# Chunk 3's decays loaded ahead of four second-layer weights, and the stored decays clipped on VectorE

## The chip, the cores and the metric

The kernel runs on one core of a Trainium2 chip. The metric is the device time of one execution in microseconds (us): 614.49 as the median of three runs (613.55, 614.49, 615.33). All arithmetic is in fp32.

The engines are named as in the profile: PE is TensorE (PEld its weight loads), DVE is VectorE, ACT is ScalarE, POOL is GpSimd, SP issues most DMAs. L625 is line 625 of the kernel before.

## The reference

The kernel computes a state-space scan over four batches of 768 positions with eight heads, and feeds its result to a layer of four gated experts. Cut to what matters here:

```python
def _attn_ref(x, a, B, C):                 # x (4, 8, 768, 32), a (4, 8, 768), B and C (4, 8, 768, 16)
    log_a = np.log(np.clip(a, 1e-06, 1.0))
    for c in range(nc):                    # chunks of the sequence
        cum = np.cumsum(la, axis=-1)
        L = np.exp(cum[:, :, :, None] - cum[:, :, None, :]) * causal
        M = np.einsum('bhin,bhjn->bhij', Cc, Bc) * L
        y = einsum('bhij,bhjd->bhid', M, xc) + einsum('bhin,bhnd->bhid', Cc, state) * exp(cum)
        state = exp(sum(la)) * state + sum_j(B_j x_j * exp(cum[-1] - cum_j))

def _moe_ref(x, domain_probs, w1, w2):     # x (3072, 256), w1 (4, 256, 1024), w2 (4, 1024, 256)
    p = domain_probs / (domain_probs.sum(-1, keepdims=True) + 1e-09)
    for e in range(E):
        out += p[:, e:e + 1] * (np.maximum(x @ w1[e], 0.0) @ w2[e])
```

`a` holds the decays that the change is about.

## The kernel before

**Tiles and stages.** The kernel works in 24 chunks of 128 positions. For each chunk it needs the matrix of decays between all pairs of positions of a head. For the first chunks this comes from a running product ("scan", L519): VectorE multiplies along the positions by the decay and adds a row of the identity. Chunks 0 to 2 spread the decays over the partitions by small matmuls into PSUM (L660) and scan from there. Chunks 3 to 5 (`c < SCANNED`) read the clipped decays from DRAM, broadcast to all 128 partitions into a 512 KB tile `ab` (`load_decays`, L463). From chunk 6 on, exponentials of cumulative sums take their place (L526). The scores of two chunks (L502, eight matmuls into four banks of PSUM) are multiplied by the decay matrices on VectorE (L856, one 128x512 product for each bank), and the outputs (L546, and L879 for the state carried from an earlier chunk) are matmuls on these products `MT`.

The expert layer follows on transposed outputs. Its products (L933) are 128x256 matmuls. The first four blocks of F use the weights as they are: `plain_first` (L1235) multiplies the first-layer weights, L968 evicts a bank through ReLU and gate, and `own_` (L1390) multiplies the second-layer weights. All other products go by schemes with fewer multiplications, for which sums of weights (L1024) are formed on GpSimd and VectorE, and sums of tokens (L1043) on VectorE.

**The beginning is written out by hand** (L560 to L738). It clips the decays of chunks 0 to 2 on VectorE (`aq0`, `aq1`), and all decays (`a_sb`, 96x256) on GpSimd. GpSimd then copies the clipped ones to `a_cut` and zeroes the first position of each row, and SP stores `a_cut` to DRAM as `acut_d` (L633). `a_sb` itself is needed later for the logarithm (L708). SP issues its DMAs in the order of the program: tokens, two first-layer weights, chunk 2's tokens, the store, chunk 3's tokens, two more first-layer weights, four second-layer weights, chunk 3's decays. The load of the decays reads what the store wrote, and SP waits for the store's completion before it issues it. A DMA also waits, at SP, for the one that last used its completion counter, some eight DMAs earlier.

**The rest is planned.** Everything from L742 on is handed to `Plan`, which walks through the work with estimated durations and sets the order of instructions on each engine. Matmuls keep the order in which the lists are written. The other engines take what is ready first by the estimates. The plan starts at `now = 13.2` us, and what the part by hand has begun enters it as "taken" with the time from which it can be used: the decays of chunk 3 (`st[3]["ab"]`, L777) at `now + 2`, the second-layer weights (L1350) at `now + 4 + fb`. Buffers, too, are given out by the plan. An instruction of GpSimd that would share a port with VectorE waits for the last two-input VectorE instruction written before it (L1515).

**The stage around the change.** TensorE's order from 12.6 us on: chunk 2's decays are spread into four banks (L660); two plain products (L933 x16 in the profile, which counts each fp32 matmul as two); a transpose of the cumulative sums (L1360); the scores of chunks 2 and 3 (L502), of which three of the four banks are banks that chunk 2's scan reads; two more plain products and the first of the second layer (L933 x24); the outputs of chunks 2 and 3 (L546). VectorE's order: four scans of chunk 2 from PSUM, an eviction L968, the first half of chunk 3's scan from `ab`, an eviction, the second half, then the four products L856 among two evictions.

Of the kernel before, what the change touches and what calls it, by code (L numbers as in the profile page):

```python
# [10 lines left out]
ALU = mybir.AluOpType  # L11
# [348 lines left out]
def kernel(  # L360
# [10 lines left out]
    nc = tc.nc  # L371

    NCH, _, W = xbc.shape
# [19 lines left out]
    def real(c):  # L393
        return c % NSEQ * NC + c // NSEQ
# [26 lines left out]
    def some(n, shape, name, pool=const):  # L421
        return [pool.tile(shape, FP32, name=f"{name}{i}") for i in range(n)]

    homes = {
        "V": some(NV - 4, [P, 2, FB], "v"),
        "W": some(NW, [P, 2 * FB], "w"),
        "bank": some(8, [P, 512], "bank", psum),
        "xb": some(4, [P, W], "xb"),
        "ab": some(2, [P, NH * P], "ab"),
        "ah": some(3, [HN, P], "ah"),  # L430
        "MT": some(2, [P, 2, NH, P + N], "MT"),
        "ctm": some(4, [HN, NT, P], "ctm"),
# [14 lines left out]
    st = {c: {} for c in range(NCH)}  # L447
# [13 lines left out]
    def load_decays(c, ab):  # L461
        src = acut_d if c < SCANNED else cum_d
        nc.sync.dma_start(  # L463
            out=ab, in_=src[real(c)].rearrange("h s -> (h s)").partition_broadcast(P))
# [10 lines left out]
    def load_w1(fb, w):  # L475
        e, f = divmod(fb, EPB)
        nc.sync.dma_start(
            out=w.rearrange("p (a f) -> p a f", a=2),
            in_=w1[e].rearrange("(a p) f -> p a f", a=2)[:, :, f * FB:f * FB + FB])

    def load_w2(fb, w):
        e, f = divmod(fb, EPB)
        nc.sync.dma_start(
            out=w.rearrange("p (j m) -> p j m", j=JJ),
            in_=w2[e, f * FB:f * FB + FB].rearrange("(j p) m -> p j m", p=P))
# [65 lines left out]
    def keep_state(c, A, y):  # L551
# [14 lines left out]
    a_sb = homes["cum"][0]  # L566
    a_cut = homes["V"][-4][:NCH * NH // 2, 0].rearrange("p (r s) -> p r s", r=2)
# [5 lines left out]
        out=aq0.rearrange("(q r) t s -> q r (t s)", q=NQ)[:, 0], in_=a_rows[:, 0])  # L573
    nc.scalar.dma_start(
        out=aq1.rearrange("(q r) c t s -> q r c (t s)", q=NQ)[:, 0], in_=a_rows[:, 1:SPREAD])
# [5 lines left out]
        out=a_sb, in_=a.rearrange("c h s -> (c h) s").rearrange("(p r) s -> p r s", r=2))  # L581
# [14 lines left out]
    for q in range(NQ):  # L596
        nc.vector.memset(tmask[32 * q:32 * q + N, 0:1], 1.0)
    nc.vector.tensor_scalar(out=tmask[:, 1:2], in0=tmask[:, 0:1], scalar1=-1.0, scalar2=1.0,
                            op0=ALU.mult, op1=ALU.add)
# [7 lines left out]
    def clip(engine, v, top=1.0):  # L607
        engine.tensor_scalar(out=v, in0=v, scalar1=1e-6, scalar2=top, op0=ALU.max, op1=ALU.min)
# [13 lines left out]
    clip(nc.vector, aq1.rearrange("p c t s -> p (c t s)"), own)  # L622
    nc.vector.memset(aq1[:, :, :, 0:1], 0.0)

    clip(nc.gpsimd, a_sb)  # L625
    nc.gpsimd.tensor_copy(a_cut, a_sb)
    nc.gpsimd.memset(a_cut[:, :, 0:1], 0.0)

    def store_decays(engine, d, sb):
        engine.dma_start(  # L630
# [3 lines left out]
    load_tokens(3, xb[3])  # L634
    for fb in range(2, 4):
        load_w1(fb, homes["W"][fb])
    for fb in range(4):
        load_w2(fb, homes["W"][4 + fb])
    load_decays(3, homes["ab"][0])

    BANK = homes["bank"]
    rows = NCH * E
# [81 lines left out]
    for r in range(2):  # L724
        nc.vector.tensor_tensor_scan(
            out=sums[:, r], data0=a_sb[:, r], data1=zeros[:NCH * NH // 2], initial=0.0,
            op0=ALU.add, op1=ALU.add)
# [14 lines left out]
    plan = Plan(homes)  # L742
    line = []
    B512, B256 = {"DVE": D512, "POOL": 1.3}, {"DVE": D256, "POOL": .72}
    now = 13.2
# [28 lines left out]
    for c, i in ((2, 2), (3, 3)):  # L774
        st[c]["xb"] = plan.taken("xb", i, now)
    st[2]["ctm"] = plan.taken("ctm", 0, now)
    st[3]["ab"] = plan.taken("ab", 0, now + 2)  # L777
    for c in range(2):
        st[c]["A"] = plan.taken("A", c, now)
    g0 = gates[0, 0] = plan.taken("gate", 0, now)  # L780
# [566 lines left out]
    loaded = {}  # L1347
    for fb in range(4):
        loaded[fb, 1] = plan.taken("W", fb, now + (0.0 if fb < 2 else 3.0))
        loaded[fb, 2] = plan.taken("W", 4 + fb, now + 4.0 + fb)  # L1350
    for (fb, l), v in loaded.items():
        weights["S", fb, l] = v

# [31 lines left out]
    for seq, _ in plain[2:]:  # L1385
        line.extend(seq)
    dma(lambda _: nc.sync.dma_start(
        out=g0.t[:, 4:6], in_=p_d[0, 4:6].rearrange("c s -> (c s)").partition_broadcast(P).rearrange(
            "p (c s) -> p c s", s=P)), kb=128, part=[g0])
# [174 lines left out]
```

## Time and profile before

| | |
|---|---|
| median of three runs | 614.49 us |
| the profiled execution's span | 615.3 us |
| TensorE busy | 605.7 us (98%) |
| VectorE busy | 489.5 us (80%) |
| ScalarE busy | 292.5 us (48%) |
| GpSimd busy | 157.6 us (26%) |
| mean granted TensorE clock | 0.997 |
| TensorE busy from 13.2 to 27.0 us | 11.74 of 13.80 us |
| TensorE busy from 27.0 to 50.0 us | 23.00 of 23.00 us |
| TensorE busy from 50.0 to 90.0 us | 38.43 of 40.00 us |
| TensorE busy from 90.0 to 605.0 us | 514.73 of 515.00 us |

The profile shows one execution. A row of its timeline has the start, the duration, the engine, the line and operation, the tiles (output, then inputs), the number of merged instructions, and in brackets how long the engine had been idle before it and what ended the idle time. A row of waits has the waiting engine and line, what released it, the sum in us, how often, and the longest. A released wait that names an engine which had long been done was for something else, often a DMA. SPq rows are the issues of DMAs by SP; when a DMA's parts have landed is in the trace as counts of its semaphore, up to 16 for each DMA.

### The profile page before, as it was taken

To read this page: it belongs to the slowest core of one execution; us is meant where nothing else is said; L and a number is where in the kernel's file an instruction comes from. 1 tells how busy PE (TensorE), PEld (TensorE's weight loads), DVE (VectorE), ACT (ScalarE), POOL (GpSimd) and SP (SyncE) were. 2 spreads that over 40 slices of the span, in tenths; PEclk is the share of its full clock that TensorE was granted. 3 is DMA by queue.
4 is the path that set the end of the run, shared out by engine and by line. 5 is a ranking of instruction groups with operands and counts; after the bars stand their busy time and mean duration, and the time that the engine had idled before them with its cause. 6 is when DMAs were issued, how large, how long until landed. Compare 5 with 4: busy or idle time off the path is not lost.

```text
span 615.3 us, 10136 instructions
## 1 busy us (share of the span) xinstructions
PE 605.7 (98%) x3365; PEld 514.8 (84%) x3365; DVE 489.5 (80%) x854; ACT 292.5 (48%) x681; POOL 157.6 (26%) x238
## 2 busy tenths in 40 slices
PE   9899999999999999999999999999999999999997
PEld 5677878888888888888888888888888888888885
DVE  7879897998969895697978988386785979576775
ACT  4237646378651327877443333844444242434441
POOL 5536556636372000776500100210000000000000
PEclk9899999999999999999999999999999999999999
DMA  7737578676863429983442424964233232964001
GB/s 249 256 114 231 204 218 300 205 224 208 280 188 94 134 34 285 297 291 146 132 144 77 137 63 118 284 222 137 61 111 87 93 90 51 303 230 126 1 0 52
DMA packets 89060, 99.65 MB, mean 162 GB/s; under 512 B 27428, under 2 KB 58928, under 8 KB 89008
## 3 DMA queue, kind: packets, MB, share of 16 engines
q1 hardware_dynamic: 88852, 98.95, 51.4%
q8 instruction: 27, 0.44, 0.3%
q14 instruction: 25, 0.20, 0.1%
q10 hardware_dynamic: 156, 0.06, 0.0%
HBM read 78.80 MB, written 20.17 MB: 161 GB/s over the span
## 4 chain that ended last, share of the span: by engine, by line
PE 92%; DVE 2%; ACT 1%; issue 0%; DVEq 0%
PE bank L933 88%; PE bank L546 2%; PE bank L502 1%; PE bank L879 1%; DVE v L960 1%; DVE v L968 1%; ACT A L556 1%; DVE MT L856 0%; ACT v L894 0%; DVE bank L1071 0%; DVE v L1260 0%; PE bank L1325 0%; DVE v L1425 0%; ACT LT L894 0%; ACT v L1330 0%
## 5 line engine op out<-in xcount | busy, mean ns | idle before, releaser
L933 PE MATMUL bank<-v,w 128*128 128x256 f32 x1716 | 402.0, 381 | 1.1 <-DVE bank L1071 0.8
L933 PEld LDWEIGHTS bank<-v,w 128*128 128x128 f32 x1716 | 325.7, 191 | 50.0 <-issue 2.9
L933 PE MATMUL bank<-Y,w 128*128 128x256 f32 x692 | 177.3, 381 | 0.7 <-ACT LT L894 0.4
L933 PEld LDWEIGHTS bank<-Y,w 128*128 128x128 f32 x692 | 130.2, 190 | 21.9 <-issue 1.7
L1213 ACT COPY v<-bank 128x512 f32<-128x512 f32 x109 | 63.9, 586 | 177.5 <-PE bank L933 165.2
L968 DVE SCALAR_TENSOR_TENSOR v<-bank,gate 128x512 f32<-128x512 f32 x147 | 101.0, 688 | 39.6 <-PE bank L933 36.8
L960 DVE TENSOR_TENSOR v<-v,v 128x512 f32<-128x512 f32 x179 | 125.9, 720 | 2.1 <-ACT v L942 0.8
L1024 POOL TENSOR_TENSOR w<-w,w 128x256 f32<-128x256 f32 x94 | 72.1, 784 | 46.0 <-DVE v L960 13.8
L1071 DVE TENSOR_TENSOR bank<-bank,v 128x512 f32<-128x512 f32 x81 | 55.5, 696 | 35.2 <-PE bank L933 23.6
L942 ACT COPY v<-bank 128x512 f32<-128x512 f32 x97 | 56.7, 587 | 55.0 <-PE bank L933 46.7
L947 ACT COPY bank<-v 128x512 f32<-128x512 f32 x126 | 73.2, 594 | 10.8 <-DVE v L968 8.7
L526 ACT ACTIVATE MT<-ab,neg 128x128 f32<-128x128 f32 x144 | 46.9, 393 | 2.0 <-DMA ab<-cum_d 2.0
L933 PE MATMUL bank<-LT,w 128*128 128x256 f32 x168 | 42.6, 380 | 0.0
L531 POOL TENSOR_SCALAR_AFFINE_SELECT MT<-MT 128x512 f32<-128x512 f32 x36 | 23.0, 652 | 67.8 <-ACT MT L526 53.9
L933 PEld LDWEIGHTS bank<-LT,w 128*128 128x128 f32 x168 | 31.8, 190 | 4.6 <-DVE v L968 0.3
L1024 POOL TENSOR_TENSOR w<-w 128x256 f32<-128x256 f32 x32 | 24.2, 762 | 23.2 <-DVE Y L1043 9.0
L960 DVE TENSOR_TENSOR v<-bank,v 128x512 f32<-128x512 f32 x26 | 17.9, 689 | 11.7 <-PE bank L933 9.9
L1260 DVE TENSOR_TENSOR v<-v,v 128x256 f32<-128x256 f32 x58 | 22.9, 431 | 1.1 <-ACT v L1213 0.7
L856 DVE TENSOR_TENSOR MT<-bank,MT 128x512 f32<-128x512 f32 x36 | 22.7, 681 | 0.1
L968 DVE SCALAR_TENSOR_TENSOR v<-v,gate 128x512 f32<-128x512 f32 x26 | 19.7, 758 | 0.4
L1213 ACT COPY LT<-bank 128x512 f32<-128x512 f32 x12 | 7.0, 586 | 23.5 <-PE bank L933 23.5
L840 POOL TENSOR_TENSOR cts<-ctm,dec 128x256 f32<-128x256 f32 x20 | 14.5, 734 | 11.6 <-DVE v L960 5.1
(110 smaller groups left out, 322.1 us busy)
## 6 DMA issues: line engine op xcount, KB each, us to landing
w<-w_d SPq DMA_DIRECT2D x128, 256.0 KB
w_d<-w SPq DMA_DIRECT2D x64, 256.0 KB
w<-in_w_dram SPq DMA_DIRECT2D x40, 256.0 KB
ab<-cum_d SPq DMA_DIRECT2D x18, 512.0 KB
w<-in_w_dram SPq DMA_DIRECT2D x64, 128.0 KB
gate<-p_d SPq DMA_DIRECT2D x15, 384.0 KB
xb<-in_xbc_dram SPq DMA_DIRECT2D x17, 192.0 KB
out_dram<-v SPq DMA_DIRECT2D x144, 16.0 KB
```

The lines of the kernel that those rows point to most:

```text
L526: nc.scalar.activation(out=MT[:, place(c, h), 0:P], in_=ab[:, h * P:h * P + P], func=AF.Exp, bias=neg[:, h % NT, NQ * real(c) + h // NT:NQ ...
L531: nc.gpsimd.affine_select(out=MT[:, h:h + n, 0:P], in_=MT[:, h:h + n, 0:P], compare_op=ALU.is_ge, fill=0.0, base=0, pattern=[[0, n], [1, P ...
L856: nc.vector.tensor_mul(to, g, LT0[:, js, h] if cs[0] < SCANNED else to)
L933: nc.tensor.matmul(out=o, lhsT=w[:, j], rhs=x if half is None else x[:, j], start=(start and j == 0), stop=(j == 1), skip_group_check=True)
L942: act(.5, lambda e: nc.scalar.copy(out=flat(v), in_=bank.t), reads=[bank], writes=[v])
L947: act(.54 if to - lo > FB else .32, lambda e: nc.scalar.copy(out=bank.t[:, lo:to], in_=flat(v)[:, lo:to]), reads=[v], writes=[bank])
L960: plan.add(engines, lambda e: (on(e).tensor_add if sign > 0 else on(e).tensor_sub)(flat(v), whole(x), whole(y)), reads=[x, y], writes=[v], ...
L968: dve(D512, lambda e: nc.vector.scalar_tensor_tensor(out=h.t, in0=whole(x).rearrange("p (j m) -> p j m", j=JJ), scalar=0.0, in1=g.t[:, 2 * ...
L1024: plan.add(B256, lambda e, r=r, x=x, y=y, sign=sign: (on(e).tensor_add if sign > 0 else on(e).tensor_sub)(view(r), view(x), view(y)), two= ...
L1071: dve(D512, lambda e: (nc.vector.tensor_add if sign > 0 else nc.vector.tensor_sub)(to.t, bank.t, whole(x)), reads=[x, bank], writes=[to])
L1213: act(.5, lambda e: nc.scalar.copy(out=flat(v), in_=bank.t), reads=[bank], writes=[v], hold=HOLD)
L1260: plan.add(engines, lambda e: (on(e).tensor_add if sign > 0 else on(e).tensor_sub)(o[1](), x[1](), y[1]()), reads=[v for v in vs if v is n ...
```

## The change

Four edits. The clip that makes `a_cut` is done on VectorE, straight from the raw decays, with the memset behind it, and GpSimd's clip in place comes after it; the copy goes. The load of chunk 3's decays stands ahead of the four second-layer weights in SP's order. In the plan, these decays are taken as there at `now` (13.2) and no longer at `now + 2`, and the second-layer weights at `now + 5 + fb` and no longer at `now + 4 + fb`.

```diff
@@ -622,9 +622,9 @@
     clip(nc.vector, aq1.rearrange("p c t s -> p (c t s)"), own)
     nc.vector.memset(aq1[:, :, :, 0:1], 0.0)
 
+    nc.vector.tensor_scalar(out=a_cut, in0=a_sb, scalar1=1e-6, scalar2=1.0, op0=ALU.max, op1=ALU.min)
+    nc.vector.memset(a_cut[:, :, 0:1], 0.0)
     clip(nc.gpsimd, a_sb)
-    nc.gpsimd.tensor_copy(a_cut, a_sb)
-    nc.gpsimd.memset(a_cut[:, :, 0:1], 0.0)
 
@@ -634,9 +634,9 @@
     load_tokens(3, xb[3])
     for fb in range(2, 4):
         load_w1(fb, homes["W"][fb])
+    load_decays(3, homes["ab"][0])
     for fb in range(4):
         load_w2(fb, homes["W"][4 + fb])
-    load_decays(3, homes["ab"][0])
 
@@ -774,7 +774,7 @@
     st[2]["ctm"] = plan.taken("ctm", 0, now)
-    st[3]["ab"] = plan.taken("ab", 0, now + 2)
+    st[3]["ab"] = plan.taken("ab", 0, now)
     for c in range(2):
@@ -1347,7 +1347,7 @@
     for fb in range(4):
         loaded[fb, 1] = plan.taken("W", fb, now + (0.0 if fb < 2 else 3.0))
-        loaded[fb, 2] = plan.taken("W", 4 + fb, now + 4.0 + fb)
+        loaded[fb, 2] = plan.taken("W", 4 + fb, now + 5.0 + fb)
```

With these numbers the plan puts VectorE's work of this stage in another order: the first half of chunk 3's scan from `ab` stands first, then two of chunk 2's scans, an eviction, the other two, an eviction, the second half of chunk 3's scan, and the four L856 among two evictions. GpSimd's first sum of weights, which waited for a VectorE sum of tokens, waits for the first half of chunk 3's scan. Later in the program neighbouring instructions change places on VectorE, ScalarE, GpSimd and SP; TensorE's order is the same, with other buffers.

## The prediction

> **What bounds the kernel now.** I read the share of each engine first, then what TensorE waited for from 13 us to the end, then the rows around the largest wait in order of time, then the busy time by stretches. The two lines from the page:
>
> ```profile
> PE 605.7 (98%) x3365; PEld 514.8 (84%) x3365; DVE 489.5 (80%) x854; ACT 292.5 (48%) x681; POOL 157.6 (26%) x238
> PE 92%; DVE 2%; ACT 1%; issue 0%; DVEq 0%
> ```
>
> TensorE is busy for 98% of the span and holds 92% of the chain that ended last. Its instructions and their order are the same in both kernels (804 rows each, buffer numbers apart), so the change can only alter its pauses. These are few:
>
> ```profile
> PE bank L546 <- POOL w L1024: 1.4, 1, 1.4
> PE bank L933 <- DVE bank L1071: 0.8, 1, 0.8
> PE bank L1325 <- DVE v L1260: 0.7, 1, 0.7
> PE bank L546 <- DVE MT L856: 0.7, 1, 0.7
> PE bank L933 <- ACT LT L894: 0.4, 1, 0.4
> PE bank L933 <- DVE v L968: 0.3, 1, 0.3
> ```
>
> Together 4.3 us, of which two rows of L546 (the outputs of chunks 2 and 3) make 2.1 us. These are what the change aims at, so no more than about 2.4 us can come from that place. The rows that lead to it:
>
> ```profile
> 6.35 0.34 SPq L630 DMA_DIRECT2D acut_d<-v  x1
> ...
> 11.23 0.47 SPq L463 DMA_DIRECT2D ab<-acut_d  x1
> ...
> 14.22 2.43 DVE L519 TENSOR_TENSOR_SCAN LT<-bank,ident 128x256 f32<-128x256 f32 x4
> ...
> 17.09 1.15 PE L502 MATMUL bank<-ctm,xb 32*128 32x256 f32 x16
> ...
> 18.17 5.45 PE L933 MATMUL bank<-v,w 128*128 128x256 f32 x24
> 19.13 1.23 DVE L519 TENSOR_TENSOR_SCAN LT<-ab,ident 128x512 f32<-128x512 f32 x1 [1.90 <-DMA ab<-acut_d]
> ...
> 25.34 0.68 DVE L856 TENSOR_TENSOR MT<-bank,LT 128x512 f32<-128x512 f32 x1
> ...
> 26.08 1.18 PE L546 MATMUL bank<-MT,xb 128*32 128x144 f32 x30 [0.70 <-DVE MT L856]
> ```
>
> Chunk 3's decays are issued at 11.23; VectorE sits idle for 1.90 us until they are there and scans at 19.13. From there it works without a gap (scan, two evictions with the scan's second half between, then four products L856 among two evictions) up to 26.02, and TensorE, ready at 18.17 + 5.45 = 23.62, starts the outputs in earnest at 26.08.
>
> **The change part by part.** Four edits.
>
> *VectorE clips the stored decays.* It adds a clip of 96x256 and a memset. Nearest rows: the clip of 128x256 at 3.22 took 0.35, the memset at 3.64 0.06. VectorE ends its own memset at 4.48 and idles 0.87 us until the scan at 5.35; the decays are there by 4.56 (the trace's landing records: the semaphore counts of the DMA engines). 4.6 + 0.4 = 5.0: hidden by that idle time, cost 0; without the cover 0.4. GpSimd loses a copy (0.39) and a memset (0.10); its own clip (1.07) now waits for VectorE's read, so it ends near 6.0 in place of 5.72, and its first reader, the logarithm, is at 8.98: cost 0, covered by 3 us.
>
> *The store of the decays* could leave SP at 5.85, where the load before it has been issued, in place of 6.35. This buys nothing: by the landing records its 16 parts land from 9.03 to 11.11, each about 0.3 us behind the load ahead of it (8.76 to 10.81), so it stands in a backlog, not on its issue.
>
> *The load is moved past four weight loads on SP.* It reads what the store wrote, so it waits for the store's 11.11. Before, SP reached it at 11.2 anyway; hence it is issued at about 11.2 in both kernels. What changes is what is ahead of it in the DMA queue: before, the four weights (the last lands at 16.35) and then the decays at 19.01; now only the first-layer weights, whose last part lands at 13.40. The landing L of the decays from both sides: other 512 KB loads of this trace land 1.2 to 2.7 us behind the transfer ahead of them, so 14.6 to 16.1; and those that found the queue nearly empty landed 3.5 (issued 288.90) to 5.1 us (265.92) after their issue, so 14.7 to 16.3. The most alike, issued with a transfer ahead that ends 2.5 us later (144.27 and 170.80), took 4.3 and 4.2. I take L = 15.4 and keep 14.6 to 16.3.
>
> The Trainium skill (DMA: Bandwidth & Descriptors, Anatomy of one DMA, fitted there on GpSimd's path) puts a DMA at some 2.0 us plus its bytes over 436 GB/s. By that the store would be done near 8.1 and the load issued there; for this store, issued at 6.35, the trace has 11.11. Since the load would still stand behind the first-layer weights, L by the page would be about 15, an estimate, and the gain 1.5 us in place of the 1.1 below.
>
> *The order on VectorE.* The planner is now told that the decays are there at 13.2, and puts the scan of their first half first, ahead of chunk 2's four scans from PSUM. That is a new wait: behind it stand the chunk 2 scans, and behind these TensorE, since the scores (L502) overwrite the banks that they read. Steps from the starts of the rows of before: landing to scan 0.12; scan 1.14; PSUM scan 0.585; eviction 0.58; second scan 1.49; L856 0.6.
> - VectorE: L + 0.12 + 1.14 + 2 x 0.585 + 0.58 + 2 x 0.585 + 0.58 + 1.49 + 2 x 0.6 + 0.6 + 0.6 + 0.68 = L + 9.35.
> - TensorE: the third scanned bank is free at L + 0.12 + 1.14 + 1.17 + 0.58 + 0.6 = L + 3.6. Five of the eight scores are left, 5/8 of 1.08, then 24 matmuls at 0.217 (a long stretch of L933 has 185.83 us for 860) make 5.2: the outputs can start at L + 9.5.
>
> Both paths are about equal; with 0.1 for the hand-over the outputs start at max(23.6, L + 9.6), that is 25.0 for L = 15.4, in place of 26.08: **1.1 us sooner** (1.9 to 0.2 over the bounds of L). Even is at L = 16.5.
>
> What else moves. SP has issued the first-layer weights by about 7.7 and now stands at the load's wait until 11.2; behind it stand four weight loads, two stores and the next tokens. The second-layer weights are issued at 11.7 to 13.5 in place of 8.23 to 11.19 and land some 2.5 us later (about 16 to 19); their first reader is the last third of the 24 matmuls, near 23 now; covered by 4 us or more. The store of the sums (12.63), the gates' store and the tokens of chunks 4 and 5 leave SP 0.5 to 1.4 us later; their readers (ACT's masks at 20.19, scores at 31.7) have cover, about 10 us up to the scores. GpSimd's first weight sum waited for a VectorE sum at 13.92 and started at 14.38; it now waits for the scan, until 16.75. Behind it stand the two L540 that the outputs need: five sums of 0.71, L540, the sum that waits for the second scan (L + 6.3 = 21.7), L540: done at 22.8, before 25.0; cost 0, and 2.2 us of cover.
>
> After this stage the plan is recomputed. On GpSimd and SP the same work is in nearly the same order; on VectorE neighbours change places. The next pauses (0.3 at 50.75, 0.8 at 77.31, 0.4 at 86.81) can shrink to nothing or double: -1.5 to +1.5, and I take 0. In the stretch from 50 to 90 us VectorE is the fullest:
>
> ```profile
> 50.00:90.00 40.00, 38.43 (x237) 31.52 (x237) 37.83 (x63) 23.16 (x68) 22.62 (x36) 1.00 0.70 216
> ```
>
> (columns: PE, PEld, DVE, ACT, POOL.) But the chain enters VectorE there at 68.36, released by a matmul, so an earlier TensorE lets it begin earlier, and the gain passes through.
>
> **The sum.** The profiled execution spans 615.3 us, 0.8 over the median of 614.49 and inside the runs shown (613.55 to 615.33). 615.3 - 1.1 = 614.2; against the median, 614.49 - 1.1 = **613.4**. Rounds of this kernel differ by 0.3% (1.8 us); below that I call it the same.
>
> **Rivals.**
> - *Faster: the later pauses go too.* With L = 14.6 the outputs gain 1.9; or the pauses at 77 and 50 us vanish besides the 1.1 (0.8 + 0.3). 614.5 - 2.2 = 612.3. For it: VectorE's products of chunks 4 and 5 come earlier in the new order (all four L856 ahead of two evictions). Against: VectorE's total work is unchanged and full in that stretch.
> - *Slower: the scan in front blocks chunk 2.* From L = 16.5 on TensorE's scores wait longer than the outputs did. If the decays land no sooner than before (19.0), the outputs start at 28.6, 2.5 us later than 26.08: 617.0. For it: this load took 7.8 us from issue to landing before, one at 77.28, with the queue almost empty, 6.65 (L = 17.9, +1.4), and the new order leaves nothing else for VectorE to do meanwhile. Against: 1 MB less is queued ahead.
> - *Given back.* VectorE is at 37.83 of 40 us from 50 to 90; if the new order makes it the bound there from 50 on, the 1.1 us are waited for again: 614.5. Against it: the release at 68.36 by TensorE.
> - *The load is not earlier at all* in its issue: that is my own forecast, and it is no rival for the time, since the queue ahead is what shrinks.
>
> **How the numbers follow.** Forecast as worked out (613.4; own range 612.6 to 614.3 by the bounds of L, up to 615.8 if later pauses grow by 1.5): 0.44. Given back (614.5): 0.08. Faster (612.3 and below): 0.30. Slower (617.0, from 616.3 on): 0.18. Same is the first two, 0.52. The range leaves out the far ends of the faster and the slower case, one in ten each: 611.7 to 616.6.
>
> **What would show it.** In the new trace: the L463 of chunk 3 issued near 11.2, not near 7.8 (else the store landed early); the first scan of `ab` on VectorE near 15.5; a new pause of TensorE at L502 of about 2 us, near 17 to 19, in place of those at L546; the outputs L546 starting at 25.0. It is wrong if the scan starts at 14 or before (then 2.4 us), if it starts after 16.5 (then slower), or if the pauses at 50 to 87 us change by more than 1 us in sum.

## The result, and the profile after

The changed kernel takes 617.46 us (median of 8 executions, 616.55 to 619.50) against 615.22 for the kernel before beside it (8 executions, 613.55 to 617.28): a ratio of 1.0038, interval 1.0021 to 1.0055. It is slower by 2.2 us, where 1.1 us less was forecast. A second comparison gave 617.32 against 614.89, ratio 1.0034 (1.0018 to 1.0050).

The profiled execution of the changed kernel spans 615.4 us, almost the 615.3 of before. From the waits of TensorE after the change (waiting engine and line, what released it, the sum in us, how often, the longest) the two rows of L546 are gone, and one of L502 has come:

```profile
PE bank L502 <- DVE LT L519: 1.0, 2, 0.6
PE bank L1325 <- DVE v L1260: 0.7, 1, 0.7
PE bank L933 <- ACT LT L894: 0.4, 1, 0.4
PE bank L933 <- DVE bank L1071: 0.3, 1, 0.3
```

TensorE pauses 1.9 us less than before, 2.4 in place of 4.3 by the rows shown, and yet nothing is won. The rows around the change, in order of time (start, duration, engine, line; in brackets the idle time before):

```profile
5.98 0.35 SPq L630 DMA_DIRECT2D acut_d<-v  x1
...
11.23 0.34 SPq L463 DMA_DIRECT2D ab<-acut_d  x1
...
16.49 1.23 DVE L519 TENSOR_TENSOR_SCAN LT<-ab,ident 128x512 f32<-128x512 f32 x1 [3.88 <-DMA ab<-acut_d]
17.10 0.69 PE L502 MATMUL bank<-ctm,xb 32*128 32x256 f32 x2
...
18.35 1.28 PE L502 MATMUL bank<-ctm,xb 32*128 32x256 f32 x4 [0.56 <-DVE LT L519]
...
20.11 1.91 PE L502 MATMUL bank<-ctm,xb 32*128 32x256 f32 x10 [0.48 <-DVE LT L519]
...
21.95 6.31 PE L933 MATMUL bank<-v,w 128*128 128x256 f32 x24
...
28.19 1.19 PE L546 MATMUL bank<-MT,xb 128*32 128x144 f32 x32
29.30 2.86 PE L933 MATMUL bank<-v,w 128*128 128x256 f32 x12
```

The load is issued at 11.23 as before, and its last part lands at 16.37 (the landing records). VectorE waits 3.88 us for it, TensorE's scores come in three pieces behind VectorE's scans, and the outputs start at 28.19, 2.1 us later than the 26.08 of before. But the ten last matmuls of the scores take 1.91 us and the next 24 take 6.31, where before all sixteen scores took 1.15 and the 24 took 5.45. The reason is in the busy time by stretches (PE, PEld, DVE, ACT, POOL, then the granted clock, the share of the DMA engines, GB/s):

```profile
16.90:20.31 3.41, 2.37 (x13) 1.16 (x13) 3.41 (x6) 0.33 (x1) 2.51 (x4) 1.00 0.90 294
20.31:23.72 3.41, 3.41 (x14) 2.39 (x14) 3.31 (x5) 1.33 (x4) 3.41 (x6) 0.50 0.78 255
```

From 20.31 to 23.72 TensorE was granted half of its clock. What takes 3.41 us there would take 1.7 at full clock. The kernel before has the same in its profiled execution, behind its pauses at the outputs, and its page shows it too (the 8 in the row of the granted clock):

```profile
23.98:27.39 3.41, 1.72 (x33) 1.23 (x34) 3.32 (x6) 0.44 (x2) 3.41 (x5) 1.00 0.83 247
27.39:30.80 3.41, 3.41 (x9) 2.70 (x9) 3.41 (x4) 1.72 (x9) 1.22 (x2) 0.50 0.60 228
```

So the two profiled executions are both charged 1.7 us, and they are equal: the outputs start 2.1 us later, 1.7 of it is made up when before's own half clock comes, and most of the rest at the pause near 77 us (L1071), which is 0.3 in place of 0.8. (The 0.33 at 50.75 is gone too, but short waits up to 57 us take it back.) What differs is how often the half clock comes. A stretch of 3.41 us at half clock lowers the mean clock of an execution by 3.41 x 0.5 / 615 = 0.003, so the mean clock that comes with every time tells the number of stretches (where in the program they lie is known for the profiled executions only):

| mean clock | stretches | before, 80 executions beside the experiments | changed kernel, 20 executions |
|---|---|---|---|
| 0.998 to 1.000 | none | 64 (613.35 to 615.78 us) | 3 (614.96 to 615.92 us) |
| 0.996 and 0.997 | one | 16 (616.77 to 617.53 us) | 11 (616.55 to 617.91 us) |
| 0.994 | two | none | 6 (618.47 to 619.57 us) |

At equal clock the kernels are less than a microsecond apart. The 2.2 to 2.4 us between the medians is mostly one stretch at half clock, which the kernel before has in one of five executions and the changed one in 17 of 20. From none to one the medians rise by 1.7 us in the changed kernel (615.5 to 617.2), as one stretch would have it, but by 2.5 in the kernel before (614.8 to 617.3); what the other 0.8 is, no run shows.

### The profile page after: what moved, and what is told of

It reads as the page before. It is cut to its first block, busy times and chain, and to the rows that moved or that the text cites. A ratio compares the mean times of both kernels' runs of the same rounds, so it can differ in the third digit from the quotient of the medians.

```text
span 615.4 us, 10138 instructions
## 1 busy us (share of the span) xinstructions
PE 607.7 (99%) x3365; PEld 515.4 (84%) x3365; DVE 488.4 (79%) x856; ACT 292.3 (47%) x681; POOL 157.9 (26%) x236
## 4 chain that ended last, share of the span: by engine, by line
PE 94%; DMA 2%; DVE 2%; ACT 1%; issue 1%; DVEq 0%
PE bank L933 89%; PE bank L502 2%; PE bank L546 2%; DMA acut_d<-v 1%; DMA ab<-acut_d 1%; PE bank L879 1%; ACT A L556 1%; PE bank L684 1%; DVE v L968 1%; DVE LT L519 0%; PE bank L660 0%; DVE v L1260 0%; PE bank L1325 0%; ACT LT L894 0%; ACT v L894 0%
## 5 line engine op out<-in xcount | busy, mean ns | idle before, releaser
L933 PE MATMUL bank<-v,w 128*128 128x256 f32 x1668 | 393.3, 381 | 0.3 <-DVE bank L1071 0.3
L933 PEld LDWEIGHTS bank<-v,w 128*128 128x128 f32 x1668 | 315.9, 190 | 48.7 <-issue 3.0
L933 PE MATMUL bank<-Y,w 128*128 128x256 f32 x692 | 177.5, 381 | 0.7 <-ACT LT L894 0.4
L933 PEld LDWEIGHTS bank<-Y,w 128*128 128x128 f32 x692 | 130.2, 190 | 22.1 <-issue 1.7
L960 DVE TENSOR_TENSOR v<-v,v 128x512 f32<-128x512 f32 x184 | 128.4, 716 | 2.3 <-ACT v L942 0.9
L1071 DVE TENSOR_TENSOR bank<-bank,v 128x512 f32<-128x512 f32 x81 | 55.5, 696 | 36.9 <-PE bank L933 25.7
L947 ACT COPY bank<-v 128x512 f32<-128x512 f32 (+1 forms) x127 | 73.4, 590 | 13.7 <-DVE v L968 11.1
L933 PE MATMUL bank<-LT,w 128*128 128x256 f32 x216 | 54.9, 379 | 0.0
L933 PEld LDWEIGHTS bank<-LT,w 128*128 128x128 f32 x216 | 41.0, 190 | 5.5
L960 DVE TENSOR_TENSOR v<-bank,v 128x512 f32<-128x512 f32 x28 | 19.3, 688 | 13.3 <-PE bank L933 10.3
L1213 ACT COPY LT<-bank 128x512 f32<-128x512 f32 x15 | 8.8, 586 | 33.6 <-PE bank L933 33.6
L856 DVE TENSOR_TENSOR MT<-bank,MT 128x512 f32<-128x512 f32 x36 | 22.8, 682 | 0.6 <-PE bank L502 0.5
L1260 DVE TENSOR_TENSOR v<-v,v 128x256 f32<-128x256 f32 x45 | 18.0, 421 | 0.6 <-ACT v L1213 0.3
L502 PE MATMUL bank<-ctm,xb 32*128 32x256 f32 x192 | 16.8, 416 | 1.4 <-DVE LT L519 1.0
```

The costliest lines, as they stand in the source:

```text
L502: nc.tensor.matmul(out=views[r][:, j], lhsT=xb[j][k, OBT:OBT + P], rhs=ctm[j][k].rearrange("p t s -> p (t s)"), start=(j == 0), stop=True, ...
L856: nc.vector.tensor_mul(to, g, LT0[:, js, h] if cs[0] < SCANNED else to)
L933: nc.tensor.matmul(out=o, lhsT=w[:, j], rhs=x if half is None else x[:, j], start=(start and j == 0), stop=(j == 1), skip_group_check=True)
L947: act(.54 if to - lo > FB else .32, lambda e: nc.scalar.copy(out=bank.t[:, lo:to], in_=flat(v)[:, lo:to]), reads=[v], writes=[bank])
L960: plan.add(engines, lambda e: (on(e).tensor_add if sign > 0 else on(e).tensor_sub)(flat(v), whole(x), whole(y)), reads=[x, y], writes=[v], ...
L1071: dve(D512, lambda e: (nc.vector.tensor_add if sign > 0 else nc.vector.tensor_sub)(to.t, bank.t, whole(x)), reads=[x, bank], writes=[to])
```

## The experiments

My theory after the result: the scan of chunk 3 in front, on which TensorE waits, costs the time, and the half clock that follows is its price; the clip and the earlier load by themselves are harmless or good. The rival: the price is the later operands or the moved load, and the clock only goes with them.

**One part at a time.** Four kernels beside before (614.93 us, 613.35 to 617.46 over 29 executions).

The clip alone:

```diff
+    nc.vector.tensor_scalar(out=a_cut, in0=a_sb, scalar1=1e-6, scalar2=1.0, op0=ALU.max, op1=ALU.min)
+    nc.vector.memset(a_cut[:, :, 0:1], 0.0)
     clip(nc.gpsimd, a_sb)
-    nc.gpsimd.tensor_copy(a_cut, a_sb)
-    nc.gpsimd.memset(a_cut[:, :, 0:1], 0.0)
```

> Of the change only the clip on VectorE. Theory (TensorE's low activity at the scores makes its clock drop, because the scan of chunk 3 stands first on VectorE): the clip has no part in it, within 0.15% of the kernel before, outputs of chunks 2 and 3 at about 26.1 us. Rival (the early store or the clip disturbs the beginning): 0.3% slower.

615.81 us, ratio 1.0015 (0.9999 to 1.0031). The store leaves SP at 5.98 in place of 6.35 and lands at 10.98, in place of 11.11. TensorE's pauses are the same. Five of 12 executions had a stretch at half clock, against 8 of 29 of before beside it; that is most of what moves the median, and it is too few to tell from chance. Read from its stretches, the fall follows the same pauses:

```profile
22.53:25.94 3.41, 1.49 (x8) 0.75 (x6) 3.41 (x6) 0.62 (x2) 3.41 (x6) 1.00 0.94 248
25.94:29.35 3.41, 3.19 (x33) 2.31 (x34) 3.32 (x5) 1.31 (x6) 2.19 (x3) 0.50 0.94 351
```

The two numbers of the plan alone, so that the scan of chunk 3 stands first and the load is where it was:

```diff
-    st[3]["ab"] = plan.taken("ab", 0, now + 2)
+    st[3]["ab"] = plan.taken("ab", 0, now)
-        loaded[fb, 2] = plan.taken("W", 4 + fb, now + 4.0 + fb)
+        loaded[fb, 2] = plan.taken("W", 4 + fb, now + 5.0 + fb)
```

> Of the change only the two numbers of the plan, so the scan of chunk 3 stands first on VectorE, while the decays land at 19.0 us as before. Theory: the scores wait until 22.7, the outputs start at about 30 (28.6 and 1.7 for a clock drop) in place of 26.1: 0.5% to 0.8% slower than before. Rival (DMA queue): nothing is moved there, the same as before.

620.97 us, ratio 1.0094 (1.0071 to 1.0117). The decays land at 18.48. In order of time:

```profile
18.60 1.22 DVE L519 TENSOR_TENSOR_SCAN LT<-ab,ident 128x512 f32<-128x512 f32 x1 [6.00 <-DMA ab<-acut_d]
...
20.46 3.83 PE L502 MATMUL bank<-ctm,xb 32*128 32x256 f32 x14 [2.67 <-DVE LT L519]
24.22 8.11 PE L933 MATMUL bank<-v,w 128*128 128x256 f32 x24
32.26 0.94 PE L546 MATMUL bank<-MT,xb 128*32 128x144 f32 x24
```

and by stretches:

```profile
15.99:19.40 3.41, 1.80 (x9) 1.12 (x7) 0.80 (x1) 0.33 (x1) 0.00 (x0) 1.00 0.97 332
19.40:29.64 10.24, 9.18 (x27) 6.59 (x28) 7.95 (x13) 1.96 (x6) 8.54 (x12) 0.50 0.59 180
```

A wait of 2.67 us is followed by three stretches of 3.41 us at half clock, and the outputs start 6.2 us later than before, at 32.26. (This is the longest of five executions, 621.27 us; the mean clock of 0.994 in the other four tells of two stretches.) The new order carries the harm.

The earlier load alone, VectorE's order as before:

```diff
+    load_decays(3, homes["ab"][0])
     for fb in range(4):
         load_w2(fb, homes["W"][4 + fb])
-    load_decays(3, homes["ab"][0])
```

> Of the change only the place of the load in SP's order; the plan's numbers and the clip as before, so chunk 2's four scans stay ahead of chunk 3's on VectorE. Theory: the decays land near 16.4 us, the scan of chunk 3 follows the eviction at about 17.2 in place of 19.13, the outputs start at about 24.2, the clock drops less often: 0.3% to 0.5% faster than before. Rival (the loss comes from the DMA queue: the second-layer weights and all behind them are late): 0.3% slower, as with the whole change.

614.65 us, ratio 0.9988 (0.9972 to 1.0003): not the 0.3 to 0.5% that I expected. None of its 12 executions had a stretch at half clock. The decays land at 16.12, and the scan of chunk 3, behind chunk 2's, starts at 17.15 without a wait. The outputs are won and lost again:

```profile
24.34 1.18 PE L546 MATMUL bank<-MT,xb 128*32 128x144 f32 x30 [0.37 <-DVE MT L856]
...
29.58 1.23 DVE L519 TENSOR_TENSOR_SCAN LT<-ab,ident 128x512 f32<-128x512 f32 x1 [1.19 <-DMA ab<-acut_d]
...
34.09 1.99 PE L933 MATMUL bank<-v,w 128*128 128x256 f32 x8 [0.96 <-DVE v L968]
```

The outputs start at 24.34 in place of 26.08, 1.7 us sooner; 10 us later TensorE pauses 0.96 us, which it did not before. There VectorE waits 1.19 us for chunk 5's decays, which take the buffer of chunk 3's. They landed at 28.78 before and at 29.48 here: the four weights that the load was moved past come later, SP issues what stands behind them later (the next tokens at 14.61, 16.14 and 17.27 in place of 14.02, 14.54 and 15.12, chunk 5's decays at 23.62 in place of 22.75), and between 2 and 31 us there is little slack to catch up in, as the DMA engines are 82% busy before and 84% here. The wait moved from chunk 3's decays to chunk 5's.

The whole change with the first number of the plan as before, so that chunk 2's scans stand first:

```diff
-    st[3]["ab"] = plan.taken("ab", 0, now)
+    st[3]["ab"] = plan.taken("ab", 0, now + 2)
```

> The whole change but the plan's number for the decays, which stays at now + 2, so chunk 2's scans stay first on VectorE. Theory: as load_only, 0.3% to 0.5% faster than before. Rival (DMA queue): 0.3% slower.

615.32 us, ratio 1.0007 (0.9990 to 1.0025). The order was what cost the time: with it undone the kernel is even with before, 3 of 12 executions with half clock. But again not faster. In the profiled execution the decays landed only at 17.40, and chunk 5's at 31.04:

```profile
24.47 1.18 PE L546 MATMUL bank<-MT,xb 128*32 128x144 f32 x30 [0.70 <-DVE MT L856]
...
35.64 1.99 PE L933 MATMUL bank<-v,w 128*128 128x256 f32 x8 [2.22 <-DVE v L968]
```

**Is it the clock or the wait?** Two kernels fill TensorE's pauses with matmuls whose result is overwritten, and one moves chunk 5's decays. They ran beside the whole change once more and before (614.89 us, 613.75 to 617.40 over 31 executions).

> The whole change once more, beside the next three kernels. Both theories: about 617.5 us, 0.3 to 0.5 % over before, and the granted clock at .994 to .997 in every execution (a full .999 to 1.000 in most of before's).

617.32 us, ratio 1.0034 (1.0018 to 1.0050); 9 of 12 executions with one stretch or two.

The whole change with its waits filled:

```diff
+        def scored(e):
+            if cs[0] == 2:
+                for _ in range(3):
+                    idle(gs_[0].t)
+            score(cs, [s["ctm"].t for s in ss], [s["xb"].t for s in ss], [b.t for b in gs_])
+
-        pe(.66 * len(cs), lambda e: score(
-            cs, [s["ctm"].t for s in ss], [s["xb"].t for s in ss], [b.t for b in gs_]),
-            reads=[s[k] for s in ss for k in ("ctm", "xb")], writes=gs_)
+        pe(.66 * len(cs), scored, reads=[s[k] for s in ss for k in ("ctm", "xb")], writes=gs_)
```

> The whole change, with three matmuls of 128 x 512 into the score bank (their result is overwritten) ahead of the scores of chunks 2 and 3, so that TensorE is busy while VectorE waits for the decays; VectorE's order and every wait stay. Theory (the scan in front starves TensorE between 17 and 20 us, and the half clock of 3.4 us that follows, at a price of 1.7 us, is what makes the change slower): the granted clock returns to .999 or 1.000 in most executions, the rest of the scores takes about 0.7 instead of 1.9 us, and the median is 1 to 2 us under the whole change's, 615.5 to 616.5. Rival (the late operands set the end, the clock only goes with them): the median stays at 617.5 or, by some of the 2.6 us that the filling takes, up to 619.

616.20 us, ratio 1.0017 to before (1.0008 to 1.0026), 1.1 us under the whole change although TensorE does 2.8 us more. All 12 executions are at a clock of 0.999 or 1.000.

```profile
16.48 2.78 PE L684 MATMUL bank<-const-float32-1.0 128*128 128x512 f32 x6
19.18 0.71 PE L502 MATMUL bank<-ctm,xb 32*128 32x256 f32 x6
20.21 1.13 PE L502 MATMUL bank<-ctm,xb 32*128 32x256 f32 x10 [0.33 <-DVE LT L519]
21.27 5.45 PE L937 MATMUL bank<-v,w 128*128 128x256 f32 x24
26.65 1.19 PE L546 MATMUL bank<-MT,xb 128*32 128x144 f32 x32
```

The decays landed no sooner (16.48) and the last scores started no sooner (20.21), yet the outputs start at 26.65 in place of 28.19, for the scores' rest takes 1.13 and the 24 matmuls 5.45. (L937 is L933 moved by four lines.) For this part the rival falls: with the same late operands, the half clock is gone and so are 1.5 us at the outputs. What is left, 1.3 us over before, comes from the later operands, the filling and a new pause of 0.24 us at 36.79; this run does not separate them.

The kernel before with its pauses at the outputs filled:

```diff
+            for w in (4, 4, 3) if cs[0] == 2 else ():
+                idle(ys[2].t, w)
             for c in cs:
                 vs[c] = v = ys[c].t
```

> The kernel before, with three matmuls (128 x 512, 512 and 384) into the bank of the outputs of chunks 2 and 3 ahead of them, where TensorE pauses from 23.6 to 26.1 us. Theory: the executions at clock .996 or .997 (7 of 29 in the last comparison, 616.8 to 617.5 us) disappear, the fastest stay at 613.4, the median falls by 0 to 0.5 us and the highest time from 617.5 to about 616. Rival (the half clock has nothing to do with these pauses): about a quarter of the executions stay at .996 to .997, and the median is the same or up to 0.5 us higher.

615.16 us, ratio 1.0002 (0.9992 to 1.0011). The median did not fall. The spread did: 614.95 to 616.16, with none of 12 executions at 0.996 or 0.997. With one in five, as in before's 80, none in 12 comes by chance in 0.8^12, 7 of 100, so this one points the same way and shows it less firmly.

Chunk 5's decays ahead of three weights, on the earlier load alone (VectorE's order and GpSimd's clip as before):

```diff
-            dma(lambda e: load_decays(c, s["ab"].t), 1, 512, part=[s["ab"]],
-                reads=[cd] if c >= SCANNED else [])
+            s["abw"] = dma(lambda e: load_decays(c, s["ab"].t), 1, 512, part=[s["ab"]],
+                           reads=[cd] if c >= SCANNED else [])
...
+    i = done.index(st[5]["abw"])
+    ws = [w for w in done[:i] if w.by == "SP"][-3:]
+    done[:i + 1] = [w for w in done[:i + 1] if w not in ws] + ws
```

> The earlier load alone (VectorE's order and GpSimd's clip as before), and the load of chunk 5's decays moved ahead of the three first-layer weights that stand in front of it on SyncE. Theory (the 1.7 us won at the outputs of chunks 2 and 3 is given back at 34 us to chunk 5's decays, which landed at 29.48 behind those weights): they land at about 27, the pause of 0.96 us at 34.09 goes to under 0.3, and the median falls by 0.5 to 1 us against the earlier load alone, to 613.7 to 614.2, 0.1 to 0.3 % under before. Rival (the weights that now come later are awaited by GpSimd's sums and TensorE): a new pause of 0.5 to 1 us after 36 us, and 614.7 or more.

613.42 us, ratio 0.9969 (0.9957 to 0.9981): faster than both kernels, by 0.3% than before. Chunk 5's decays land at 27.06 and not at 29.48; their scan follows without a wait, and the pause at 34 us is gone:

```profile
24.35 1.18 PE L546 MATMUL bank<-MT,xb 128*32 128x144 f32 x30 [0.36 <-DVE MT L856]
...
28.32 2.33 DVE L519 TENSOR_TENSOR_SCAN LT<-ab,ident 128x512 f32<-128x512 f32 x2
...
29.32 5.79 PE L933 MATMUL bank<-v,w 128*128 128x256 f32 x24
35.04 0.66 PE L879 MATMUL bank<-cts,S 32*32 32x256 f32 x16
```

Against the earlier load alone this is 1.2 us, for a pause of 0.96: the give-back is explained. Once more, with and without the clip on VectorE (before: 615.04 us, 613.52 to 617.53 over 20 executions):

> The earlier load with chunk 5's decays ahead of three weights, once more: 613.0 to 613.7 us, 0.2 to 0.4 % under before, no execution under clock .998. If the first comparison was luck: within 0.1 % of before.

613.56 us, ratio 0.9967 (0.9955 to 0.9980), no execution under 0.998.

> The same with VectorE clipping the stored decays in place of GpSimd. Theory (the clip alone is worth nothing, as the store waits in the backlog of loads in either case): within 0.3 us of the kernel beside it. Rival (the clip alone, which stood at 1.0015 with an interval that just holds 1, has a cost of its own through VectorE's earlier or later scans): 0.6 to 1 us more, 614.0 to 614.4.

613.57 us, ratio 0.9979 (0.9966 to 0.9992). The medians agree to 0.01 us, so by them the clip is worth nothing in this place. Two of its 12 executions took 614.88 and 615.87 at full clock; in the latter, which was profiled, TensorE paused 1.41 us ahead of 29.73, behind ScalarE, which had waited for a load of cumulative sums that landed at 28.04. Whether the clip makes that more likely stays open.

## Why the prediction was wrong, step by step

- **"The change can only alter its pauses"**: this is the step that failed. The sum counted TensorE's pauses and left out its clock. It had two consequences. The new wait of the scores was priced at its idle time, though 1.7 us of slow matmuls follow it. And the profiled span of 615.3, against which the sum was made, held 1.7 us at half clock which four of five executions of before don't have.
- **The landing L.** Forecast 15.4, bounds 14.6 to 16.3. It was 16.37 and, over all eight profiled executions with the load in this place, 15.45 to 17.40. The forecast missed by 1.0; the latest of the eight lies 1.1 above the upper bound. It came 3.0 us behind the last first-layer weight (13.38), where other rows had shown 1.2 to 2.7 us from one transfer to the next.
- **The path on VectorE and TensorE.** "The outputs start at L + 9.6" was short by 0.5: without half clock the outputs started 6.44 us after the start of the last ten scores (20.21 to 26.65), where 5.9 had been put. From start to start these took 1.06 and not 0.68, and the 24 matmuls 5.38 and not 5.2. (VectorE's steps as listed add up to L + 9.33, not 9.35; nothing hangs on it.) The whole miss then adds up: 25.0 forecast, + 1.0 for the landing, + 0.5 for the scores, + 1.7 for the clock = 28.2, and 28.19 was measured.
- **"A new pause of TensorE at L502 of about 2 us"**: the rows show 0.56 and 0.48, as scores that could run stand between them. The delay is at the last ten scores, which start at 20.11.
- **The clip hidden, the store's earlier issue worth nothing, the load issued at about 11.2**: right. The store left SP 0.37 us earlier and landed at 11.21 in place of 11.11; the load went out at 11.23.
- **GpSimd's first sum waits until 16.75, cost 0**: the wait was there (17.80) and cost nothing that TensorE's waits show.
- **The Trainium skill's rule for one DMA** (DMA: Bandwidth & Descriptors, Anatomy of one DMA), by which the store would be done near 8.1: the trace disagrees. That rule was fitted on GpSimd's path; this store, issued by SP, takes 5.2 us from issue to last landing here, and 4.1 to 5.3 over the other profiled executions.
- **Later pauses unchanged in sum, -1.5 to +1.5**: they fell by 0.8, inside the bounds.
- **The slower rival** named the right place and mechanism (the scan in front blocks chunk 2), with a threshold of L = 16.5 that this L just missed. By its pricing the change should have been even; the clock made the difference. With the decays at their old landing it gave 28.6 for the outputs, and the two plan numbers alone gave 32.26.

The forecast gain itself was there: 1.7 us at the outputs with the earlier load alone. It took VectorE's old order to get it, and chunk 5's decays moved up to keep it.

## What to carry to other kernels

Add the granted clock to a sum of TensorE's time: look first whether the profiled execution holds a stretch at half clock, and price a new pause with the slow stretch that may follow it. Where several executions differ by a fixed step, their mean clocks tell whether it is this. And in a stretch where the DMA engines have little slack, a load that is moved up pushes the others back: find the next one that somebody waits for, and order that one too.

## What the runs showed of the hardware

In the profiled executions every fall of the clock that was not at the end of the program lasted 3.41 us, or three times that (10.24), at exactly half. This agrees with the Trainium skill (TensorE: Matmul & The Clock Gate, Part 1), which gives a free-running window of 3413 ns. For the rise at a kernel's start it says that the moment depends on where in the window the first matmul lands. Carried over to the falls, which is an inference, that would explain why the clock falls in 16 of before's 80 executions and not in the others; no trace shows an execution of before without the fall, so its pauses may also have been shorter.

Against the advice on the same page of the Trainium skill to avoid idle gaps of more than about 3 us (HAM oscillation, and the table of why this matters), much shorter pauses were enough: 1.36 and 0.70 us in before, 0.56 and 0.48 in the changed kernel. In the 3.41 us ahead of the fall TensorE was busy for 1.72, 1.49, 1.80 and 2.37 us in the executions shown, and in the repeat of the changed kernel for 2.92, most of it scores, which use 32 of the 128 rows:

```profile
18.17:21.58 3.41, 2.92 (x17) 1.82 (x18) 3.41 (x6) 0.09 (x1) 3.41 (x6) 1.00 0.72 239
21.58:24.99 3.41, 3.41 (x10) 2.70 (x9) 2.63 (x5) 1.61 (x5) 3.41 (x6) 0.50 0.70 212
```

The busy times overstate the work. The end of a matmul is modelled, and a score by itself counts 0.37 to 0.48 us at full clock, where sixteen in a row take 1.15: the 2.92 us hold 17 matmuls. Nor does the busy time alone decide. With chunk 2's scans first, the pause of 2.22 us ahead of 35.64 brought no fall in its profiled execution, though TensorE was busy for only 1.90 us from 31.53 to 34.95, with nine matmuls of 128x256 on all 128 rows. What the gate counts, whether matmuls on 32 rows count for less, and from which share of a window it acts, stays open.
